# Attention scores from 64-row halves: Q and K turned in float32 two heads at a time, split after the turn

## The chip, the cores and the metric

The kernel runs on one core of a Trainium2 chip. The metric is device time in microseconds, from the profiler's records of whole executions; the median of several runs is compared.

## The reference, cut to what matters

Three stages follow each other: windowed attention with a few sink tokens, a dense feed-forward layer (FFN), and a routed layer of 8 experts.

```python
batch, n_heads, seq, head_dim = (2, 8, 768, 64)
n_sink, window = (4, 128)
scores = scale * np.matmul(q, k.transpose(0, 1, 3, 2))
keep = is_sink | in_window
scores = np.where(keep, scores, -1000000000.0)
scores = scores - np.max(scores, axis=-1, keepdims=True)
a = np.exp(scores)
a = a / (np.sum(a, axis=-1, keepdims=True) + 1e-09)
attn_out = np.matmul(a, v)
x = attn_out.transpose(0, 2, 1, 3).reshape(B * S, H * D)
h = x @ w_in
x = np.maximum(0.01 * h, h) @ w_out
```

Behind it every one of the 1536 tokens goes to the expert of its largest gate logit, while that has room. The weights of the FFN and the experts come as float64.

## The kernel before, in words

**Tiles.** The 1536 tokens are 12 tiles `t` of 128 (6 for each batch entry; `i = t % 6`). Heads go in groups `g` of 4 (two a tile) and in pairs `pr` of 2 (two a group). A score tile of one head holds the keys of the tile itself, of the one before, and of the 4 sinks: `kT` keeps two slots of 128 keys and 4 sink keys each, 264 columns. Tiles 0 and 1 go a plain way of their own (`qk_plain`, `scores_plain` and so on, L624 to L712); tiles 2 to 11 go through `RingAttention` (L394), and of them speaks the change.

**Products in two parts.** To multiply in fp32r, the kernel splits a number into a high part (a copy to fp32r) and a low part (the number less its high part), and sums products of parts. Before the change `high_k` and `low_k` (L146, L151) split K as it lies in memory and put both parts of a head side by side, 64 + 64 columns; `trans_k` (L157) turns these by TensorE (`kps`), so the high part lies on the upper and the low part on the lower 64 rows of `kT`. `high_q`, `low_q` and `trans_q` (L171 to L202) do the same for Q, in both orders, high above low and low above high: for `t < EARLY` (4) by turning 8 tiles a group (`qps`), from there on by turning 4 and copying the halves across on VectorE (L202). `scores` (L487) then needs two matmuls for a head, each over all 128 rows:

```python
for vv in range(2):
    nc.tensor.matmul(out, lhsT=self.qT[t, g][vv][:, h, :], rhs=rhs, start=(vv == 0), stop=(vv == 1))
```

Behind the scores come a copy on ScalarE (`pm`, L506), the window's part on VectorE (L513), the maximum `mx` (L514), exps (L219), the norm (`ri`, L226; POOL, L229), transposes (`pps`, L536) and the product with V: `pv` (L558), where the heads of a pair write the upper and the lower 64 partitions of one PSUM tile in turn, so that each matmul uses 64 columns of the array (`128*64` in the rows; the others say `128*128`).

**What sets the order.** `pipeline` (L333) lays the parts of a group and of a pair on steps: `high_q` and `high_k` three steps ahead of the scores, the low parts two ahead, the turns one ahead, exps one behind, `trans` four and `pv` five behind. From tile 2 on a pair takes two steps. `build` puts these steps between the FFN's work on blocks `j` of 256 tokens: `first` (`hps`, L841), a step, `second` (`y`, L887). Tiles 2, 3 and the start of tile 4 run beside block 0; for that block the FFN uses float32 weights, and VectorE converts 16 weight chunks from float64 (`word`, `cvt`: L779, L783, L789) while DMAs bring them (`rawi`, `rawo`). TensorE, ScalarE, POOL and SP (which issues the DMAs) keep the order of the code. VectorE's order is set by the scheduler that builds the program.

**Buffers.** `kps`, `qps`, `sps` (one a head), `pps` and `ops` take turns in 4 PSUM buffers of tag `att`; a tile is turned into a buffer only when its reader four tiles back is through.

Of the kernel before, what the change touches and what calls it, by code (L numbers as in the profile page):

```python
# [18 lines left out]
P = 128  # L19
# [374 lines left out]
class RingAttention(Attention):  # L394
# [16 lines left out]
    def setup(self):  # L411
        nc = self.nc
        c = self.p["ac"]
        self.R = 2
        self.SC = (self.n_sink + 1) // 2 * 2
        SC = self.SC
        self.W = P + SC
        self.kT = [c.tile([P, self.G, 2, self.W], F32R, name=f"kT{g}") for g in range(self.NG)]
        fill = NEG
        self.qk, self.mp = {}, []  # L420
        if self.plain:
            self.ident_b = self.p["c"].tile([P, P], BF16, tag="c", name="ident_b")
            nc.vector.tensor_copy(self.ident_b, self.ident)
        for t in range(self.plain):

            m = self.p["c"].tile([P, (t + 1) * P], BF16, tag="c", name="mp")
            nc.gpsimd.memset(m, 0.0)
            for x in range(t + 1):
                self.keep_mask(m[:, x * P:(x + 1) * P], (t - x) * P, 0 if x else self.n_sink, fill)
            self.mp.append(m)  # L430
            for g in range(self.NG):
                q = self.p["c"].tile([P, 2, P], F32, tag="c", name="qp")
                k = self.p["c"].tile([P, 2, 2, P], F32, tag="c", name="kz")
                for e in range(2):
                    nc.vector.memset(k[64 - 64 * e:128 - 64 * e, e], 0.0)
                self.qk[t, g] = q, k

        self.m0 = c.tile([P, P], F32, name="m0")
        nc.gpsimd.memset(self.m0, 0.0)
        self.keep_mask(self.m0, 0, self.n_sink, fill)  # L440
        if SC:


            self.m1 = c.tile([P, SC], F32, name="m1")
            self.m2 = c.tile([P, SC], F32, name="m2")
            for m in (self.m1, self.m2):
                nc.gpsimd.memset(m, 0.0)
                if self.n_sink < SC:
                    nc.gpsimd.memset(m[:, self.n_sink:], fill)
            nc.gpsimd.affine_select(out=self.m1, in_=self.m1, pattern=[[-1, SC]],  # L450
                                    compare_op=ALU.is_ge, fill=fill, base=0, channel_multiplier=1)

        self.both = c.tile([P, 2, P], F32, name="both")
        for m, v in ((self.both[:, 0], 1.0), (self.both[:, 1], 0.0)):
            nc.gpsimd.memset(m, v)
            nc.gpsimd.affine_select(out=m, in_=m, pattern=[[1, P]], compare_op=ALU.is_ge, fill=1.0 - v,
                                    base=0, channel_multiplier=-1)

        self.sel = c.tile([P, P], F32, name="sel")
        nc.gpsimd.memset(self.sel, 1.0)  # L460
        nc.gpsimd.affine_select(out=self.sel, in_=self.sel, pattern=[[-1, P]], compare_op=ALU.is_ge, fill=0.0,
                                base=0, channel_multiplier=1)
        self.vs = {}
        if SC:
            self.psk = [c.tile([P, 4, 32], F32, name=f"psk{n}") for n in range(2)]
            for t in self.psk:
                nc.gpsimd.memset(t, 0.0)

    def sink_load(self, b):
# [7 lines left out]
                              in_=self.A["v"][b, e::2, 0:SC, :].rearrange("h s d -> s h d"))  # L477
        self.vs[b] = raw

    def tile_start(self, t):  # L480
        b, i = divmod(t, self.NT)
        if t == self.plain - 1:
            self.load(t + 1, "kqv")
        if self.SC and (b or not self.plain) and self.NT > 1 and i == 0:
            self.sink_load(b)

    def scores(self, t, g, pr):  # L487
        nc = self.nc
        b, i = divmod(t, self.NT)
        W = self.W  # L490
        pm = self.p["pp"].tile([P, 2, W], F32, tag="pm", name="pm")
        mx = self.p["sm"].tile([P, 2], F32, tag="mx", name="mx")
        own = i % 2
        w = W if i else P
        sps = [self.p["ps"].tile([P, 2, W], F32, tag="att", name="sps") for e in range(2)]
        for e in range(2):
            h = 2 * pr + e
            rhs = self.kT[g][:, h, :, :] if i else self.kT[g][:, h, 0, 0:P]
            out = sps[e] if i else sps[e][:, 0, 0:P]
            for vv in range(2):  # L500
                nc.tensor.matmul(out, lhsT=self.qT[t, g][vv][:, h, :], rhs=rhs, start=(vv == 0), stop=(vv == 1))  # L501
        for e in range(2):
            if i == 0:
                nc.vector.tensor_tensor(out=pm[:, e, 0:P], in0=sps[e][:, 0, 0:P], in1=self.m0, op=ALU.add)
            else:
                nc.scalar.copy(pm[:, e, :], sps[e][:, 1 - own, :])  # L506
        if i == 1 and self.SC or i > 1 and self.n_sink < self.SC:
            m = self.m1 if i == 1 else self.m2
            nc.vector.tensor_tensor(out=pm[:, :, P:], in0=pm[:, :, P:],
                                    in1=m.unsqueeze(1).to_broadcast([P, 2, self.SC]), op=ALU.add)  # L510
        if i:
            for e in range(2):
                nc.vector.copy_predicated(pm[:, e, 0:P], self.sel.bitcast(I32), sps[e][:, own, 0:P])  # L513
        nc.vector.reduce_max(mx, pm[:, :, 0:w], axis=AX.X, negate=True)  # L514
        self.pu[t, g, pr] = (pm, mx, w)
# [66 lines left out]
    def steps(self, dense):  # L582

        n, first = self.first_steps()
        return self.pipeline(range(self.plain, self.B * self.NT), dense, n, first,
                             (self.high_k, self.low_k, self.trans_k, self.prep_v))


    def first_steps(self):
# [23 lines left out]
                out.append((u + PT + 1, 0, None, a[0]))  # L613

        for g in range(NG):
            s = base + 2 * g * self.G // 2
            for x in ([0] if self.SC else []) + [self.plain - 1]:
                out += [(s - 3, 0, self.high_k, x, g), (s - 2, 0, self.low_k, x, g), (s - 2, 1, self.trans_k, x, g)]
            out.append((s + 1, 0, self.prep_v, self.plain - 1, g))
        if self.SC:  # L620
            out.append((SINK, 0, self.sink_load, 0))
        return base, out
# [1 line left out]
    def qk_plain(self, t, g):  # L624


        nc = self.nc
        ps = self.p["ps"].tile([P, 4, P], F32, tag="att", name="kps")
        for n, (nm, pr) in enumerate(("kq"[n // 2], n % 2) for n in range(4)):
            x = self.heads(t, g, nm)[:, 2 * pr:2 * pr + 2, :]  # L630
            nc.tensor.transpose(ps[:, n, :], x.rearrange("p a d -> p (a d)"), self.ident)
        q, k = self.qk[t, g]
        nc.vector.tensor_copy(k[0:64, 0], ps[0:64, 0:2, :])
        nc.scalar.copy(k[64:128, 1], ps[64:128, 0:2, :])
        nc.scalar.activation(q, ps[:, 2:4, :], AF.Copy, scale=self.scale)

    def scores_plain(self, t, g):

# [1239 lines left out]
```

## Time and profile before

| | us |
|---|---|
| median of 3 runs | 616.04 |
| lowest and highest run | 615.83, 618.12 |
| the profiled execution, its own time | 618.46 |
| span of its instructions | 616.5 |
| TensorE busy in the span | 586.6 |
| VectorE busy | 382.7 |
| ScalarE busy | 311.9 |
| POOL busy | 179.2 |

PE is TensorE's matmuls and PEld its weight loads, which run beside them; DVE is VectorE, ACT ScalarE. A matmul's row gives a modelled end, and matmuls overlap in the pipeline: what one costs is read from one start to the next. Attention lies between the start and 376 us, the FFN's six blocks between 37 and some 425 us, the experts behind.

### The profile page before, as it was taken

Reading aid. Unit: us, or ns where it says so; the run is one execution under the profiler, and the core shown is the slowest. Engines: PE = TensorE matmul, PEld = TensorE weight load, DVE = VectorE, ACT = ScalarE, POOL = GpSimd, SP = SyncE. Lnnn points to the kernel's source line nnn. Section 1 sums busy time; section 2 is a strip of 40 time slices with the busy share of each in tenths; the row PEclk is TensorE's granted clock in tenths of the full one; section 3 lists DMA queues with packets and bytes.
Section 4 is the critical chain, followed back from the end, with each engine's and each line's share of the span. In section 5 each row is a group of like instructions: output and inputs, shape, how many; then the busy total and the mean of one; then the engine's idle time right before and its main releaser. Section 6 shows DMA issues by size and latency. Waiting matters only on the chain.

```text
span 616.5 us, 11665 instructions
## 1 busy us (share of the span) xinstructions
PE 586.6 (95%) x3889; PEld 502.4 (81%) x3889; DVE 382.7 (62%) x928; ACT 311.9 (51%) x920; POOL 179.2 (29%) x328
## 2 busy tenths in 40 slices
PE   7698998999999999999999999999999999999994
PEld 7575665689889888998889988988798989998783
DVE  4789998377854555555655542266456676655992
ACT  4665555576655455545555433254244544444772
POOL 4425555633342224332422232223110120102110
PEclk9899999999999999999999999999969999999998
DMA  9769989622653402330223015755165856643950
GB/s 244 185 206 249 294 231 269 158 83 53 226 185 108 115 19 69 87 103 19 61 58 98 1 48 164 259 183 165 59 207 172 259 177 204 195 133 111 304 188 12
DMA packets 83564, 91.88 MB, mean 149 GB/s; under 512 B 42964, under 2 KB 51156, under 8 KB 83473
## 3 DMA queue, kind: packets, MB, share of 16 engines
q1 hardware_dynamic: 81488, 85.68, 47.1%
q0 software_dynamic: 1984, 5.13, 2.3%
q8 instruction: 39, 0.64, 0.4%
q14 instruction: 53, 0.43, 0.2%
HBM read 72.01 MB, written 20.09 MB: 149 GB/s over the span
## 4 chain that ended last, share of the span: by engine, by line
PE 70%; DVE 13%; DMA 7%; issue 7%; ACT 3%; POOL 0%; another core or an unknown queue 0%; POOLq 0%; SPq 0%; ACTq 0%; DVEq 0%
PE y L887 18%; PE hps L841 17%; PE ph L1306 10%; PE py L1355 8%; PE ops L568 4%; DVE cvt L789 3%; PE sps L501 3%; DMA out<-ys,gt 2%; DVE word L779 2%; DVE word L783 2%; DMA craw<-in_moe_w 2%; PE lps L972 2%; PE sps L652 1%; PE pps L536 1%; PE kps L163 1%
## 5 line engine op out<-in xcount | busy, mean ns | idle before, releaser
L887 PE MATMUL y<-wh,gp 128*128 128x512 f32 x320 | 115.9, 403 | 0.7 <-ACT gp L867 0.7
L869 POOL TENSOR_TENSOR gp<-g,gp 128x256 fp32r<-128x256 f32 x77 | 56.8, 738 | 197.3 <-ACT gp L867 172.3
L841 PE MATMUL hps<-xth,wh 128*128 128x256 f32 x320 | 92.8, 290 | 0.0
L841 PE MATMUL hps<-xtl,wh 128*128 128x256 f32 x320 | 90.1, 281 | 0.0
L841 PE MATMUL hps<-xth,wl 128*128 128x256 f32 x320 | 89.9, 281 | 0.0
L1170 DVE TENSOR_TENSOR cw<-craw,cw 128x512 fp32r<-128x512 f32 x128 | 83.4, 695 | 9.1 <-ACT cw L1168 7.9
L1168 ACT CAST cw<-craw 128x512 fp32r<-128x512 f32 x112 | 63.4, 621 | 23.7 <-PE py L1355 22.3
L887 PEld LDWEIGHTS y<-wh,gp 128*128 128x128 f32 x320 | 60.0, 188 | 14.3 <-issue 2.7
L857 ACT ACTIVATE g<-hps 128x256 f32<-128x256 f32 x80 | 30.6, 382 | 70.0 <-PE hps L841 65.7
L1355 PE MATMUL py<-cw,ht 128*128 128x512 f32 x264 | 63.9, 397 | 0.2 <-DVE ht L1343 0.2
L841 PEld LDWEIGHTS hps<-xth,wh 128*128 128x128 f32 x320 | 60.3, 188 | 3.3 <-issue 0.9
L841 PEld LDWEIGHTS hps<-xtl,wh 128*128 128x128 f32 x320 | 60.3, 188 | 3.1 <-issue 0.7
L887 PE MATMUL y<-wl,gp 128*128 128x512 f32 x160 | 62.7, 392 | 0.0
L1306 PE MATMUL ph<-xt,cw 128*128 128x256 f32 (+2 forms) x444 | 62.3, 304 | 0.4 <-issue 0.4
L1306 PEld LDWEIGHTS ph<-xt,cw 128*128 128x128 f32 x444 | 61.1, 204 | 0.7 <-issue 0.5
L841 PEld LDWEIGHTS hps<-xth,wl 128*128 128x128 f32 x320 | 60.6, 189 | 0.0
L1355 PEld LDWEIGHTS py<-cw,ht 128*128 128x128 f32 x264 | 49.1, 189 | 11.5 <-DVE ht L1343 0.7
L858 DVE TENSOR_TENSOR g<-hps,g 128x256 f32<-128x256 f32 x80 | 33.4, 418 | 25.6 <-ACT g L857 25.3
L219 ACT ACTIVATE pm<-pm,mx 128x132 f32<-128x132 f32 (+1 forms) x80 | 31.7, 398 | 29.1 <-DVE mx L514 28.9
L867 ACT CAST gp<-g 128x256 fp32r<-128x256 f32 x80 | 33.3, 416 | 23.8 <-DVE g L858 23.6
L1364 POOL DMA_INDIRECT out<-ys,gt x11 | 11.4, 1036 | 114.7 <-DVE ys L1363 114.7
L543 DVE TENSOR_TENSOR pt<-pps,both 128x512 f32<-128x512 f32 x28 | 19.3, 688 | 35.7 <-PE pps L538 35.7
(211 smaller groups left out, 1121.0 us busy)
## 6 DMA issues: line engine op xcount, KB each, us to landing
craw<-in_moe_w SPq DMA_DIRECT2D x128, 256.0 KB, 3.5
rawi<-in_moe_w_in SPq DMA_DIRECT2D x16, 512.0 KB, 5.0
rawo<-in_moe_w_out SPq DMA_DIRECT2D x16, 512.0 KB, 5.4
places<-zero SPq DMA_DIRECT2D x24, 257.0 KB, 5.7
wh<-wscr SPq DMA_DIRECT2D x16, 256.0 KB, 2.9
wl<-wscr SPq DMA_DIRECT2D x16, 256.0 KB, 3.4
xg<-places SPq DMA_DIRECT2D x12, 257.0 KB, 4.4
natv<-in_v SPq DMA_DIRECT2D x12, 256.0 KB, 5.2
```

Of the source, the lines that this page charges most:

```text
L219: nc.scalar.activation(pm[:, e, 0:w], pm[:, e, 0:w], AF.Exp, bias=mx[:, e:e + 1], accum_out=su[:, e:e + 1])
L568: nc.tensor.matmul(ps[64 * e:64 * e + 64, :], lhsT=l, rhs=r, start=(x == 0), stop=(x == len(mm[0]) - 1))
L841: nc.tensor.matmul(ps, lhsT=w, rhs=x, start=(n == 0), stop=(n == len(mm) - 1))
L857: nc.scalar.activation(g, ps, AF.Copy, scale=0.01)
L858: nc.vector.tensor_tensor(out=g, in0=ps, in1=g, op=ALU.max)
L867: nc.scalar.copy(gp[:, 0], g)
L869: eng.tensor_tensor(out=gp[:, 1], in0=g, in1=gp[:, 0].bitcast(F32), op=ALU.subtract)
L887: nc.tensor.matmul(y, lhsT=l, rhs=r, start=(start and n == 0), stop=(stop and n == len(mm) - 1))
L1168: nc.scalar.copy(h, t)
L1170: eng.tensor_tensor(out=l, in0=t, in1=h.bitcast(F32), op=ALU.subtract)
L1306: nc.tensor.matmul(self.ph[f][:, sl], lhsT=self.w[e, "a", h, k][w][:, f * P:(f + 1) * P], rhs=self.xt[:, a, k, sl], start=(m == 0), stop=( ...
L1355: nc.tensor.matmul(self.py[n], lhsT=x, rhs=w, start=(h == 0 and f == 0 and m == 0), stop=(h == self.NH - 1 and f == self.HF - 1 and m == 2))
```

## The change

Q and K of two heads (64 + 64 columns) are turned together in float32, so that one head of a pair lies on the upper and the other on the lower 64 rows. Both are split behind the turn, out of PSUM, into high and low: `qT` holds both parts of a group in one tile, `kT` becomes a high and a low tensor, kTh and kTl. `trans_q` does all of it; `high_k`, `low_k` and `trans_k` are no longer called in the ring, `high_q` does nothing, `low_q` only issues the next load. The scores of a head are three products (high by high, high by low, low by high), each over the head's 64 rows, the two heads in turn. The keys of tile 1 and the sinks of tile 0 are kept from the plain way's own transposes; the second copy of the sinks is made on POOL.

```diff
--- before.py
+++ after.py
@@ -415,7 +415,8 @@
         self.SC = (self.n_sink + 1) // 2 * 2
         SC = self.SC
         self.W = P + SC
-        self.kT = [c.tile([P, self.G, 2, self.W], F32R, name=f"kT{g}") for g in range(self.NG)]
+        self.kT = [[c.tile([P, self.G // 2, 2, self.W], F32R, name=f"kT{a}{g}") for a in "hl"]
+                   for g in range(self.NG)]
         fill = NEG
         self.qk, self.mp = {}, []
         if self.plain:
@@ -477,6 +478,42 @@
                               in_=self.A["v"][b, e::2, 0:SC, :].rearrange("h s d -> s h d"))
         self.vs[b] = raw
 
+    def high_q(self, t, g):
+        pass
+
+    def low_q(self, t, g):
+        if g == self.NG - 1:
+            self.load(t + 1, self.WITH_Q)
+
+    def keep_k(self, t, g, ps):
+
+        nc, SC, i = self.nc, self.SC, t % self.NT
+        hi, lo = ([k[:, :, i % 2, 0:P]] + [k[:, :, r, P:] for r in range(2 if i == 0 and SC else 0)]
+                  for k in self.kT[g])
+        for n, (h, l) in enumerate(zip(hi, lo)):
+            if n == 2:
+                nc.gpsimd.tensor_copy(h, hi[1].bitcast(F32))
+                nc.gpsimd.tensor_copy(l, lo[1].bitcast(F32))
+            elif n or t >= self.plain - 1:
+                src = ps[:, :, 0:SC] if n else ps
+                nc.scalar.copy(h, src)
+                nc.vector.tensor_tensor(out=l, in0=src, in1=h.bitcast(F32), op=ALU.subtract)
+
+    def trans_q(self, t, g):
+
+        nc, NP = self.nc, self.G // 2
+        ps = self.p["ps"].tile([P, 2, NP, P], F32, tag="att", name="qps")
+        for a, nm in enumerate("qk"):
+            for pr in range(NP):
+                x = self.heads(t, g, nm)[:, 2 * pr:2 * pr + 2, :]
+                nc.tensor.transpose(ps[:, a, pr, :], x.rearrange("p a d -> p (a d)"), self.ident)
+        qT = self.p["c"].tile([P, 2, NP, P], F32R, tag="c", name="qT")
+        nc.scalar.activation(qT[:, 0], ps[:, 0], AF.Copy, scale=self.scale)
+        nc.vector.scalar_tensor_tensor(out=qT[:, 1], in0=ps[:, 0], scalar=self.scale, in1=qT[:, 0].bitcast(F32),
+                                       op0=ALU.mult, op1=ALU.subtract)
+        self.qT[t, g] = qT
+        self.keep_k(t, g, ps[:, 1])
+
     def tile_start(self, t):
         b, i = divmod(t, self.NT)
         if t == self.plain - 1:
@@ -493,12 +530,12 @@
         own = i % 2
         w = W if i else P
         sps = [self.p["ps"].tile([P, 2, W], F32, tag="att", name="sps") for e in range(2)]
-        for e in range(2):
-            h = 2 * pr + e
-            rhs = self.kT[g][:, h, :, :] if i else self.kT[g][:, h, 0, 0:P]
-            out = sps[e] if i else sps[e][:, 0, 0:P]
-            for vv in range(2):
-                nc.tensor.matmul(out, lhsT=self.qT[t, g][vv][:, h, :], rhs=rhs, start=(vv == 0), stop=(vv == 1))
+        for n, (a, c) in enumerate(((0, 0), (0, 1), (1, 0))):
+            for e in range(2):
+                r = slice(64 * e, 64 * e + 64)
+                k = self.kT[g][c][r, pr]
+                nc.tensor.matmul(sps[e] if i else sps[e][:, 0, 0:P], lhsT=self.qT[t, g][r, a, pr, :],
+                                 rhs=k if i else k[:, 0, 0:P], start=(n == 0), stop=(n == 2))
         for e in range(2):
             if i == 0:
                 nc.vector.tensor_tensor(out=pm[:, e, 0:P], in0=sps[e][:, 0, 0:P], in1=self.m0, op=ALU.add)
@@ -583,7 +620,7 @@
 
         n, first = self.first_steps()
         return self.pipeline(range(self.plain, self.B * self.NT), dense, n, first,
-                             (self.high_k, self.low_k, self.trans_k, self.prep_v))
+                             (None, None, None, self.prep_v))
 
 
     def first_steps(self):
@@ -613,10 +650,7 @@
                 out.append((u + PT + 1, 0, None, a[0]))
 
         for g in range(NG):
-            s = base + 2 * g * self.G // 2
-            for x in ([0] if self.SC else []) + [self.plain - 1]:
-                out += [(s - 3, 0, self.high_k, x, g), (s - 2, 0, self.low_k, x, g), (s - 2, 1, self.trans_k, x, g)]
-            out.append((s + 1, 0, self.prep_v, self.plain - 1, g))
+            out.append((base + 2 * g * self.G // 2 + 1, 0, self.prep_v, self.plain - 1, g))
         if self.SC:
             out.append((SINK, 0, self.sink_load, 0))
         return base, out
@@ -633,6 +667,8 @@
         nc.vector.tensor_copy(k[0:64, 0], ps[0:64, 0:2, :])
         nc.scalar.copy(k[64:128, 1], ps[64:128, 0:2, :])
         nc.scalar.activation(q, ps[:, 2:4, :], AF.Copy, scale=self.scale)
+        if t == self.plain - 1 or t == 0 and self.SC:
+            self.keep_k(t, g, ps[:, 0:2])
 
     def scores_plain(self, t, g):
```

On TensorE, a group's turn and its first scores (tile 4's first group, in the FFN's block 0; ops is `pv`, hps and y the FFN). Before:

```order
L568 MATMUL ops<-pt,natv 64x128 x4
L568 MATMUL ops<-sp,vsraw 64x128 x2
L163 MATMUL kps<-ident_r,ks 128x128 x4
L197 MATMUL qps<-ident_r,qs 128x128 x4
L841 MATMUL hps<-xth,cvt 128x256 x4
L536 MATMUL pps<-ident,pm 128x128 x2
L538 MATMUL pps<-ident,psk_195 128x128
L501 MATMUL sps<-kT_125,qT 128x264 x4
L887 MATMUL y_723<-cvt,gr 128x512
```

With the change:

```order
L605 MATMUL ops<-pt,natv 64x128 x4
L605 MATMUL ops<-sp,vsraw 64x128 x2
L509 MATMUL qps<-ident,natq 128x128 x2
L509 MATMUL qps<-ident,natk 128x128 x2
L877 MATMUL hps<-xth,cvt 128x256 x4
L573 MATMUL pps<-ident,pm 128x128 x2
L575 MATMUL pps<-ident,psk_197 128x128
L537 MATMUL sps<-kTh_125,qT 128x264 x2
L537 MATMUL sps<-kTl_126,qT 128x264 x2
L537 MATMUL sps<-kTh_125,qT 128x264 x2
L923 MATMUL y_681<-cvt,gr 128x512
```

Four turns of K and four of Q become two of each in float32, and the four score matmuls over all rows are six, in three couples; the rest keeps its place.

Where the ring begins on TensorE (tile 2, behind the plain way's last pv). Before:

```order
L163 MATMUL kps<-ident_r,ks 128x128 x8
L708 MATMUL ops<-pt,natv 64x128 x8
L163 MATMUL kps<-ident_r,ks 128x128 x4
L197 MATMUL qps<-ident_r,qs 128x128 x8
L841 MATMUL hps<-xth,cvt 128x256 x4
L501 MATMUL sps<-kT_125,qT 128x264 x4
```

With the change:

```order
L744 MATMUL ops<-pt,natv 64x128 x8
L509 MATMUL qps<-ident,natq 128x128 x2
L509 MATMUL qps<-ident,natk 128x128 x2
L877 MATMUL hps<-xth,cvt 128x256 x4
L537 MATMUL sps<-kTh_125,qT 128x264 x2
L537 MATMUL sps<-kTl_126,qT 128x264 x2
L537 MATMUL sps<-kTh_125,qT 128x264 x2
```

The turns of K for tiles 0, 1 and 2 and eight of Q become two of Q and two of K; the FFN's first matmuls follow directly.

On VectorE, around the first scores of tile 3 (pm, mx and ri belong to the pair before; word and cvt convert weights). Before:

```order
L779 TENSOR_SCALAR word<-rawo 128x512
L513 COPY_PREDICATED pm<-sel,sps 128x128 x2
L783 SCALAR_TENSOR_TENSOR word<-rawo,word 128x512
L514 TENSOR_REDUCE mx<-pm 128x2
L226 TENSOR_SCALAR ri<-su 128x2
L577 TENSOR_TENSOR xtl<-ops,xth 128x128
L227 RECIPROCAL ri<-ri 128x2
L789 SCALAR_TENSOR_TENSOR cvt<-rawo,word 128x512
L779 TENSOR_SCALAR word<-rawi 128x512
L783 SCALAR_TENSOR_TENSOR word<-rawi,word 128x512
L789 SCALAR_TENSOR_TENSOR cvt<-rawi,word 128x512
```

With the change:

```order
L815 TENSOR_SCALAR word<-rawo 128x512
L550 COPY_PREDICATED pm<-sel,sps 128x128 x2
L819 SCALAR_TENSOR_TENSOR word<-rawo,word 128x512
L551 TENSOR_REDUCE mx<-pm 128x2
L226 TENSOR_SCALAR ri<-su 128x2
L825 SCALAR_TENSOR_TENSOR cvt<-rawo,word 128x512
L512 SCALAR_TENSOR_TENSOR qT<-qps,qT 128x256
L614 TENSOR_TENSOR xtl<-ops,xth 128x128
L227 RECIPROCAL ri<-ri 128x2
L815 TENSOR_SCALAR word<-rawi 128x512
L500 TENSOR_TENSOR kTl_126<-qps,kTh_125 128x2x128
L819 SCALAR_TENSOR_TENSOR word<-rawi,word 128x512
```

The low part of Q (qT) now stands behind the conversion that follows ri, and the low part of K (kTl) behind another; these scores need both. Before, no row of VectorE here belonged to them.

## Rows read from the trace of the kernel before

**Rows 1.** The page, part 1: busy us (share of the span) x instructions, by engine.

```profile
PE 586.6 (95%) x3889; PEld 502.4 (81%) x3889; DVE 382.7 (62%) x928; ACT 311.9 (51%) x920; POOL 179.2 (29%) x328
```

**Rows 2.** Busy time by stage: stretch, its us, then busy us of each engine.

```profile
34.00:106.00 72.00, 63.36 (x361) 44.17 (x358) 64.20 (x129) 40.72 (x136) 34.13 (x53) 1.00 0.90 257
...
130.00:205.00 75.00, 75.00 (x570) 66.79 (x569) 49.08 (x134) 44.78 (x146) 26.13 (x42) 1.00 0.41 130
```

**Rows 3.** The chain that ended last, 20 to 108 us: start us, us, what.

```profile
28.47 0.91 ACT ks L149 x3
...
29.38 0.54 ACT qs L175
...
69.47 0.89 ACT pm L219 x4
...
71.52 0.71 DVE word L779
...
104.95 0.69 DVE qT L202
...
106.40 0.64 PE sps L501 x3
```

**Rows 4.** Waits of PE, 28 to 130 us: us in total, times, longest.

```profile
PE qps L197 <- DVE pm L513: 5.1, 4, 2.5
```

**Rows 5.** PE by line and shape: xcount | busy us, mean ns | idle before.

```profile
L501 PE MATMUL sps<-kT,qT 128*128 128x264 f32 x144 | 27.8, 310 | 2.5 <-DVE qT L202 1.0 <-ACT qT L199 0.9
...
L197 PE MATMUL qps<-ident_r,qs 128*128 128x128 f32 x96 | 11.7, 250 | 5.1 <-DVE pm L513 5.1
```

**Rows 6.** PE in order of time, a score step: start us, us, instruction, count.

```profile
228.80 0.38 PE L536 MATMUL pps<-ident,pm 128*128 128x128 f32 x2
...
229.04 0.73 PE L501 MATMUL sps<-kT,qT 128*128 128x264 f32 x4
229.61 0.39 PE L887 MATMUL y<-wh,gp 128*128 128x512 f32 x1
229.84 0.40 PE L887 MATMUL y<-wl,gp 128*128 128x512 f32 x1
```

**Rows 7.** PE in order of time, a pv step.

```profile
224.52 0.28 PE L841 MATMUL hps<-xtl,wh 128*128 128x256 f32 x1
224.64 0.28 PE L841 MATMUL hps<-xth,wl 128*128 128x256 f32 x1
224.85 0.66 PE L568 MATMUL ops<-pt,natv 128*64 128x128 f32 x8
225.34 0.39 PE L568 MATMUL ops<-sp,vsraw 128*64 128x128 f32 x4
225.65 0.50 PE L887 MATMUL y<-wh,gp 128*128 128x512 f32 x1
225.99 0.40 PE L887 MATMUL y<-wl,gp 128*128 128x512 f32 x1
```

**Rows 8.** PE in order of time, a group's transposes and the y behind them.

```profile
233.33 0.53 PE L163 MATMUL kps<-ident_r,ks 128*128 128x128 f32 x4
...
234.04 0.46 PE L887 MATMUL y<-wh,gp 128*128 128x512 f32 x1
234.34 0.39 PE L887 MATMUL y<-wl,gp 128*128 128x512 f32 x1
```

**Rows 9.** DVE by line and shape: xcount | busy us, mean ns.

```profile
L858 DVE TENSOR_TENSOR g<-hps,g 128x256 f32<-128x256 f32 x80 | 33.4, 418 | 25.6 <-ACT g L857 25.3
...
L182 DVE SCALAR_TENSOR_TENSOR qs<-natq,qs 128x256 fp32r<-128x256 f32 x20 | 9.1, 456 | 1.5 <-ACT qs L175 1.5
```

**Rows 10.** PE in order of time, tile 3's first scores and the y behind.

```profile
71.53 1.12 PE L501 MATMUL sps<-kT,qT 128*128 128x264 f32 x4
72.48 0.59 PE L887 MATMUL y<-cvt,gr 128*128 128x512 f32 x1
```

**Rows 11.** PEld in order of time, the weight loads of that pv step.

```profile
224.84 0.42 PEld L568 LDWEIGHTS ops<-pt,natv 128*64 128x64 f32 x8
```

## The prediction

> **What bounds the kernel now.** I read first the page's busy shares: TensorE is busy for 586.6 of 616.5 us [rows 1]. That is an average, so next the table by stage, where the reader should compare TensorE's busy time with the length of each stretch [rows 2]. From 130 us on it fills the stretch (75.00 of 75.00): there each ns of its queue is a ns of the kernel. From 34 to 106 us it is busy for 63.36 of 72. The chain that ended last says why [rows 3]: in that first stage the chain runs through VectorE, which converts the raw weights (word and cvt steps of some 0.7 us) and does attention between them; at 106.40 us it passes to TensorE (sps). The table of waits names one TensorE wait that matters to the change: 5.1 us in four pieces, qps waiting for a PSUM buffer that VectorE's pm step has not yet released [rows 4].
>
> So the change has two prices: on TensorE's queue after 106 us (10 tiles are turned here, 2 to 11; of their 40 pair steps the 32 of tiles 4 to 11, of their 20 groups the 15 from tile 4's second on), and on VectorE's before that.
>
> **Scores, on TensorE.** The 160 score matmuls (144 of 264 columns and 16 of 128 [rows 5]) become 240, 6 in place of 4 for each pair. What 4 cost: the first transpose starts at 228.80, the first y at 229.61; three transposes of 0.11 (two take 0.38, the last of them 0.27) leave 0.48 us, 0.12 each [rows 6]. The 6 new ones come as three couples, one on the upper and one on the lower 64 rows. No row shows row halves. The nearest is pv, where couples use the left and right 64 columns of the array: 8 matmuls start at 224.85 and the next 4 at 225.34, so after a first couple of 0.16 each couple takes 0.11, which is the time of one matmul [rows 7]. I take couples to overlap by rows as they do by columns: 3 times 0.12, **-0.12 us** a pair.
>
> The same rows show the price of changing the array's shape. Whole-array matmuls of that line come each 0.12 us, but from the last one (224.64) to pv's first it is 0.21; pv's last two couples and the way out take 0.31 (225.34 to 225.65) where two couples would take 0.22; and the first y lasts 0.34 to the next, not 0.23 [rows 6, 7]. All in all 224.64 to 225.99 is 1.35 us for 0.12 + 6 x 0.11 + 0.23 = 1.01: **0.34 us for one visit**, 0.09 on the way in and 0.09 on the way out in which nothing starts, the rest weights whose load is not hidden (0.05 for 64 columns in, 0.11 for 128 out). The new couples load 128 columns each, so in becomes 0.11 too and a visit 0.40. Today's scores pay nothing of this, since transposes, scores and y all use the whole array. Bounds: 0 (row halves need no change of shape) to 0.40; I take 0.40, as the row nearest in kind shows it at every visit.
>
> Here a rule speaks against the change. The Trainium skill, "TensorEngine Tiling (Array Packing)", Tiling Modes, Key Properties, says that changing the tiling mode, rows included, drains the engine. For columns the trace agrees (the 0.21 and the 0.31 above); for rows no run here shows it. By that rule the sum is the one below; without it, the first rival's.
>
> Sum for scores after 106 us: 32 x (0.40 - 0.12) = **+9.0 us**.
>
> **Transposes, on TensorE.** Today a group of 4 heads turns 8 tiles (4 kps, 4 qps; 12 while t is under 4, and k of tiles 0 and 1 as well; 96 are qps [rows 5]). From the first kps to the y behind them it takes 233.33 to 234.04, and that y lasts 0.30, not 0.23 [rows 6, 8]: 0.78 us. The change turns two heads at once in float32, 4 tiles of 0.11 as the pm transposes of [rows 6], which lengthen nothing behind them; with the 0.03 of the way out of pv that stays, 0.47. **15 x -0.31 = -4.7 us.** The extra k turns of tiles 0 and 1 lie before 37 us and belong to the next part.
>
> **The first stage.** There VectorE counts. Gone: the q split (20 x 0.456 us), for t of 4 and more the k split and the two half copies of qT (0.69 each in the chain [rows 3]). New: q and k are both split out of PSUM, 256 columns each; L858, which reads PSUM in the same shape, takes 0.42 [rows 9]. So each of the three groups from tile 2's second to tile 3 gives VectorE 2 x 0.42 - 0.456 = 0.38 more, +1.2 us. At tile 4's first group 1.39 of half copies on the chain are replaced by 0.84 plus, by the new order, part of a 0.7 conversion that now stands ahead of the two splits: -0.4 at best. At the start ks, qs and the q split (0.91 + 0.54 [rows 3], 0.46 [rows 9]) leave the chain; the raw weights' DMA is late next, so I count 1.9 less at most. Together **-1.1 us**. The 5.1 us of TensorE's waits for a PSUM buffer go as well (one buffer a group in place of two or three), but they are not added: TensorE would only arrive sooner at a VectorE that is itself the bound. There is also a new wait: couples 2 and 3 need the low k, and in the new order conversion, q split, word and k split follow the exps (69.47 + 0.89 us [rows 3]), which lets the second couple of tile 3's scores start at some 73.2 us, where all four matmuls began at 71.53 and the y behind them at 72.48 [rows 10]. With two couples more, y comes at some 73.7, 1.2 later. Behind that wait stand y and hps, which have the 5.1 us to give. Bounds of the stage: -4 (all the start's gain, some of the waits) to +3 (the new wait three times at 1.2, nothing gained).
>
> ScalarE loses work in every group, and POOL the early k splits; no engine but TensorE is waited for after 130 us [rows 2], so that is worth nothing. Input DMAs and SP's order stay as they are.
>
> **Sum.** +9.0 - 4.7 - 1.1 = **+3.2 us**. Against the profiled execution's own 618.46 us that is 621.7; that execution lies 2.4 above the median of the three runs, 616.04, against which the forecast is **619.2 us**. A measurement of this kernel can tell about 0.5% (3.1 us) from no change, so this case lies just on that line.
>
> **Rivals.**
> First, *row halves cost no change of shape* (**606 us**, the other side). Place: in and out of every score step. If the weights of a half load behind a whole-array matmul, the visit costs 0 and the sum is 32 x -0.12 - 4.7 - 1.1 = -9.6. It decides from a visit under 0.22 us: there the total falls 3 us below today's. For it: both halves of the rows still feed all 128 columns, unlike pv's couples. Against it: 0.34 at every visit of [rows 7]. Between the two, *only the empty 0.09 in and 0.09 out*, with loads hidden: 32 x 0.06 = +1.9, total -3.9, **612 us**.
>
> Second, *the couples do not overlap* (**630 us**): the change does not do what its order promises. Six matmuls at 0.12 make 0.72, so 32 x (0.72 + 0.40 - 0.48) = +20.5, total +14.7. A milder form has the same price: a half's next weights wait until its matmul is through, a couple takes 0.11 + 0.12 = 0.23, three 0.69, total +13.7. For it: row halves write the same PSUM partitions, which pv's column halves do not. Against it: pv's loads, 8 in 0.42 us, run ahead of their matmuls, 8 in 0.66 [rows 7, 11]. The milder form is how the Trainium skill, "TensorE: Matmul & The Clock Gate", Part 3, The mechanism, puts it: a weight load overlaps a running matmul only when the row groups differ. The column couples here contradict it as a general rule, since their loads overlap on all rows.
>
> Third, *VectorE's first stage* goes to its bounds: +3 makes the forecast 623, -4 makes it 616.
>
> **How the numbers follow.** Forecast with full price of shape 0.50, half of it (the first stage decides) beyond the 0.5% line. No price 0.17; only the empty time 0.18, two thirds of it faster by over 0.5%; no overlap 0.13; an unforeseen gain 0.02. Faster: 0.17 + 0.11 + 0.02 = 0.30. Same: 0.25 + 0.07 = 0.32. Slower: 0.25 + 0.13 = 0.38. The range goes from the first rival with a little of the first stage, 605, to 627, above the forecast's upper bound of 623 and short of no overlap at all. The forecast's own range is 615 to 623.
>
> **What would show it.** Score couples starting together and three in 0.36 us: the overlap is right. From the last transpose to the first couple 0.2 and from first y to second 0.34: the price of shape is right; 0.11 and 0.23: the first rival. Four transposes in 0.44 us. In the first stage the waits of qps for pm gone and waits of sps for VectorE's kTl in their place. Wrong would be the whole argument if TensorE no longer filled the stretches after 130 us, or if the stage before 106 us moved by more than 4 us.

## The result, and the profile after

The changed kernel takes **620.63 us** (median of 11 runs, 618.4 to 624.42) against 616.47 (11 runs, 614.57 to 618.12): ratio 1.007, 95% interval 1.005 to 1.0089. Forecast was 619.2, with 605 to 627 as its range; the result is slower by 0.7%, with an interval that begins at 0.5%. Slower was the likeliest of the three cases, if narrowly.

The profiled execution of the change is one of its shortest (span 616.8 us, own time 618.51), that of the kernel before one of its longest (span 616.5). So their ends lie 0.3 us apart where the medians lie 4.2 apart, and the two traces are compared stretch by stretch.

The page's busy shares of the change (the line that answers to [rows 1]):

```profile
PE 584.9 (95%) x3857; PEld 488.7 (79%) x3857; DVE 362.0 (59%) x906; ACT 290.5 (47%) x868; POOL 172.3 (28%) x328
```

VectorE, ScalarE and POOL each have less to do (VectorE 20.7 us less), and TensorE is as full as before: the kernel did not become shorter by what the side engines were spared.

Busy time by stage, the stretches of [rows 2]: stretch, its us, busy us of PE, PEld, DVE, ACT and POOL, then TensorE's granted clock, DMA share and GB/s.

```profile
34.00:106.00 72.00, 64.21 (x331) 41.79 (x332) 60.71 (x133) 33.64 (x119) 31.44 (x50) 0.95 0.87 260
130.00:205.00 75.00, 75.00 (x562) 64.33 (x561) 45.22 (x132) 40.59 (x138) 25.71 (x42) 1.00 0.45 138
```

From 130 us on TensorE still fills the stretch, so the sum on its queue is the right sum there. TensorE in order of time, the score step that answers to [rows 6] (start us, us, instruction, count):

```profile
227.82 0.38 PE L573 MATMUL pps<-ident,pm 128*128 128x128 f32 x2
228.04 0.27 PE L575 MATMUL pps<-ident,psk 128*128 128x128 f32 x1
228.25 0.39 PE L537 MATMUL sps<-kTh,qT 64*128 64x264 f32 x2
228.47 0.29 PE L537 MATMUL sps<-kTl,qT 64*128 64x264 f32 x2
228.60 0.28 PE L537 MATMUL sps<-kTh,qT 64*128 64x264 f32 x2
228.81 0.50 PE L923 MATMUL y<-wh,gp 128*128 128x512 f32 x1
229.14 0.40 PE L923 MATMUL y<-wl,gp 128*128 128x512 f32 x1
```

From the first transpose to the second y it takes 229.14 - 227.82 = 1.32 us, where it took 229.84 - 228.80 = 1.04: **+0.28 a pair**, the forecast's 0.40 - 0.12. (Over all 30 score steps behind the start of block 1, read from the last transpose to the second y, the mean is +0.26.) The pieces are those of the forecast: 0.21 into the first couple, couples 0.12 apart once the first is through, 0.33 from first y to second.

The turns of a group and the y behind them, same view (they answer to [rows 8]):

```profile
232.61 0.44 PE L509 MATMUL qps<-ident,natq 128*128 128x128 f32 x2
232.89 0.38 PE L509 MATMUL qps<-ident,natk 128*128 128x128 f32 x2
233.02 0.47 PE L923 MATMUL y<-wh,gp 128*128 128x512 f32 x1
233.34 0.39 PE L923 MATMUL y<-wl,gp 128*128 128x512 f32 x1
```

0.41 to the y, and that y lasts 0.32, 0.09 more than 0.23: 0.50 us for 0.78, **-0.28 a group** (forecast -0.31).

Waits of TensorE from 34 to 106 us (us in total, times, longest; [rows 4] held 5.1 us of qps waiting for pm):

```profile
PE sps L537 <- ACT kTh L499: 5.4, 4, 4.3
PE hps L877 <- ACT gr L889: 1.6, 1, 1.6
PE sps L537 <- DVE kTl L500: 0.6, 2, 0.3
```

The wait for pm is gone and a wait for k stands in its place, as foreseen; but it is mostly for the *high* part, which ScalarE writes, and 4.3 us of it come in one piece, at the scores of tile 2's second group.

### The profile page after: what moved, and what is told of

The parts are those of the page before. It is cut to its first block, busy times and chain, and to the rows that moved or that the text cites. A ratio compares the mean times of both kernels' runs of the same rounds, so it can differ in the third digit from the quotient of the medians.

```text
span 616.8 us, 11516 instructions
## 1 busy us (share of the span) xinstructions
PE 584.9 (95%) x3857; PEld 488.7 (79%) x3857; DVE 362.0 (59%) x906; ACT 290.5 (47%) x868; POOL 172.3 (28%) x328
## 5 line engine op out<-in xcount | busy, mean ns | idle before, releaser
L923 PE MATMUL y<-wh,gp 128*128 128x512 f32 x320 | 119.1, 413 | 0.6 <-ACT gp L903 0.6
L1342 PE MATMUL ph<-xt,cw 128*128 128x256 f32 (+2 forms) x444 | 59.3, 295 | 1.1 <-DVE xt L1330 1.1
L1342 PEld LDWEIGHTS ph<-xt,cw 128*128 128x128 f32 x444 | 58.0, 194 | 1.4 <-DVE xt L1330 1.3
```

The lines of the kernel that those rows point to most:

```text
L923: nc.tensor.matmul(y, lhsT=l, rhs=r, start=(start and n == 0), stop=(stop and n == len(mm) - 1))
L1342: nc.tensor.matmul(self.ph[f][:, sl], lhsT=self.w[e, "a", h, k][w][:, f * P:(f + 1) * P], rhs=self.xt[:, a, k, sl], start=(m == 0), stop=( ...
```

## The experiments

Times are medians beside the kernel before on the same chip (616.9 to 617.4 there). Sums over the whole kernel also depend on the granted clock that an execution had in its first 34 us and among the experts, so below some runs are compared at equal mean granted clock. This holds only for edits that leave the clock of the stretches between as it is. For the change these are 618.4 and 618.51 us at 0.987 to 0.988, 620.28 to 621.18 at 0.982 to 0.983 and 624.11 and 624.42 at 0.976.

**e1_by_head: are couples side by side?**

```diff
-        for n, (a, c) in enumerate(((0, 0), (0, 1), (1, 0))):
-            for e in range(2):
+        for e in range(2):
+            for n, (a, c) in enumerate(((0, 0), (0, 1), (1, 0))):
```

> The change with its two score loops exchanged: head by head instead of couple by couple, so that matmuls on the same 64 rows follow each other and nothing else differs. Theory (two matmuls on different rows run side by side): three couples 0.12 us apart become six starts 0.11 to 0.12 us apart, +0.36 us a pair on a full TensorE, 32 pairs: +11.5, some 632 us (1.025 of the kernel before). Rival (the couples were never side by side, their common start in the trace is only how it is recorded): the time stays at 620 to 621 us.

Measured: 623.85 us (4 runs), but at equal clock 622.02 at 0.980 and 623.55 to 624.15 at 0.977, where the change had 622.12 at 0.980 and 624.11 at 0.976: the same, the rival's time. But its reason need not follow. TensorE in order of time, a score step of this kernel:

```profile
205.88 0.38 PE L573 MATMUL pps<-ident,pm 128*128 128x128 f32 x2
206.19 0.40 PE L537 MATMUL sps<-kTh,qT 64*128 64x264 f32 x2
206.42 0.29 PE L537 MATMUL sps<-kTl,qT 64*128 64x264 f32 x2
206.54 0.29 PE L537 MATMUL sps<-kTh,qT 64*128 64x264 f32 x2
206.76 0.50 PE L923 MATMUL y<-wh,gp 128*128 128x512 f32 x1
```

The program has kTh, kTl, kTh of one head and then of the other. The trace has kTh kTh, kTl kTl, kTh kTh, the two of each couple 10 ns apart, in 35 of the 40 steps: TensorE drew the second head's matmuls forward beside the first's. Only around waits does the order of the program show, as at 55 us, where the second matmul waited for kTl and nothing was drawn past it:

```profile
55.48 0.58 PE L537 MATMUL sps<-kTh,qT 64*128 64x264 f32 x1 [4.27 <-ACT kTh L499]
56.07 0.58 PE L537 MATMUL sps<-kTl,qT 64*128 64x264 f32 x1
56.08 0.80 PE L537 MATMUL sps<-kTh,qT 64*128 64x264 f32 x2
```

So by these records the halves of the rows start side by side in either order of the loops, and this test could not tell the theories apart; e2_padded and e6_neighbours together can.

**e2_padded: the same six matmuls without a change of shape.** k's parts are stored for each head on all 128 rows, zeros on the other head's 64:

```diff
-        self.kT = [[c.tile([P, self.G // 2, 2, self.W], F32R, name=f"kT{a}{g}") for a in "hl"]
+        self.kT = [[c.tile([P, 2, self.G // 2, 2, self.W], F32R, name=f"kT{a}{g}") for a in "hl"]
...
-                r = slice(64 * e, 64 * e + 64)
-                k = self.kT[g][c][r, pr]
-                nc.tensor.matmul(sps[e] if i else sps[e][:, 0, 0:P], lhsT=self.qT[t, g][r, a, pr, :],
+                k = self.kT[g][c][:, e, pr]
+                nc.tensor.matmul(sps[e] if i else sps[e][:, 0, 0:P], lhsT=self.qT[t, g][:, a, pr, :],
```

> The change with k's high and low parts of both heads kept on all 128 rows, the other head's 64 rows zero, so that the same six matmuls use the whole array and the array never changes shape for the scores; no two of them can then run side by side. Theory (a visit of another shape costs 0.39 us): six times 0.12 = 0.72 us in place of 0.36 + 0.39 = 0.75, 32 pairs: -1, and the k split in twice as many pieces gives VectorE up to +2 in the first stage: 619 to 622 us; last transpose to first score 0.11 us, first y to second 0.23. Rival (the 0.39 has nothing to do with the shape, it comes with the tiles or their weights): it stays, the couples are lost, +0.36 x 32 = +11.5, some 632 us.

Measured: 625.77 us (4 runs), between the two. A score step of it, same view:

```profile
228.91 0.38 PE L577 MATMUL pps<-ident,pm 128*128 128x128 f32 x2
229.13 0.27 PE L579 MATMUL pps<-ident,psk 128*128 128x128 f32 x1
229.16 0.49 PE L541 MATMUL sps<-kTh,qT 128*128 128x264 f32 x2
229.49 0.40 PE L541 MATMUL sps<-kTl,qT 128*128 128x264 f32 x2
229.73 0.41 PE L541 MATMUL sps<-kTh,qT 128*128 128x264 f32 x2
229.98 0.39 PE L927 MATMUL y<-wh,gp 128*128 128x512 f32 x1
230.21 0.39 PE L927 MATMUL y<-wl,gp 128*128 128x512 f32 x1
```

From the first transpose to the second y: 1.30 us, against 1.32 of the change. The six come one by one, 0.12 apart, and with the whole array y follows y in 0.23 again: 0.36 of lost couples are paid for by 0.39 of shape (-0.03 forecast, -0.02 measured). By itself this step would also fit couples that never overlapped and a change of shape that is free (0.72 against 0.75); e6_neighbours rules that out. The missing 5 us lie elsewhere: the first hps is at 40.77 us (35.98 in the change, 38.05 in e1_by_head), and block 1 begins at 129.10 (119.49 and 121.91). Zeros have to be written there and four pieces of k split; that these are the cause was not tested. From there to the last y it takes 311.57 us, in the change 312.94.

**e3_f32_whole: nothing split.**

```diff
-        for n, (a, c) in enumerate(((0, 0), (0, 1), (1, 0))):
-            for e in range(2):
...
+        for e in range(2):
+            k = self.kT[g][:, e, pr]
+            nc.tensor.matmul(sps[e] if i else sps[e][:, 0, 0:P], lhsT=self.qT[t, g][:, pr, :],
+                             rhs=k if i else k[:, 0, 0:P], start=True, stop=True)
```

> Turned in float32 as in the change, but nothing is split: q and k stay float32, k of both heads on 128 rows with the other head's rows zero, two whole-array float32 matmuls of 264 columns a pair. A float32 matmul of 256 columns (hps from cvt, first stage) starts 0.216 us after the last, so 264 columns take 0.22. Theory (price of the shape 0.39): 0.44 us in place of 0.75, 32 x -0.31 = -9.8, and VectorE is rid of the q split and half of the k work in the first stage, -1 to -2: 609 to 611 us, faster than both kernels. Rival (no price for the shape): 0.44 for 0.36 + 0.39 that stays, +2.6, less the first stage: some 621 to 623 us.

Measured: 627.27 us (4 runs). My price was wrong, not the theory of the shape:

```profile
227.86 0.38 PE L573 MATMUL pps<-ident,pm 128*128 128x128 f32 x2
228.08 0.27 PE L575 MATMUL pps<-ident,psk 128*128 128x128 f32 x1
228.19 1.06 PE L537 MATMUL sps<-kT,qT 128*128 128x264 f32 x4
228.89 0.59 PE L923 MATMUL y<-wh,gp 128*128 128x512 f32 x1
229.31 0.39 PE L923 MATMUL y<-wl,gp 128*128 128x512 f32 x1
```

Two float32 matmuls leave *four* records 0.22 apart: one costs 0.45 us, four times the 0.11 of a rounded one. The 0.216 I had taken from hps<-cvt was half of such a matmul; the records there (128 for 64 matmuls of the program) had told it. With 4 x 0.22 the step is 1.45 us, and 0.11 + 0.89 + 0.23 from the last transpose to the second y (229.31 - 228.08 = 1.23) leaves nothing for a change of shape. The Trainium skill, "FP8 and Floating Point Precision", TensorE Precision Notes, gives true float32 four passes through the array; the 0.45 against 0.11 agrees. Block 1 to the last y takes 315.57 us, 2.6 more than in the change. The experts behind it took 189.7 us in place of 184.4 in this run; the mean granted clock there was 0.967 in place of 0.976, which over that time makes up for 1.7 us by my estimate, and the rest I cannot explain.

**e4_early_turn: the wait of the first stage.** On ScalarE the copy to qT and the high k stand behind the exps; turned one step earlier they stand ahead.

```diff
-                put(mid, s - 1, self.trans_q, t, g)
+                put(mid, s - (2 if t < 5 else 1), self.trans_q, t, g)
```

> The change with the turns of q and k of tiles 2 to 4 issued one step earlier, so that on ScalarE the copy to qT and the high k stand ahead of the exps and do not wait for VectorE's mx. Theory (ScalarE's order makes TensorE's new wait of 4.3 us at 49 to 53 us, and the fall of the granted clock to 0.66 in 50 to 60 us comes from it): the wait of sps for kTh goes, the clock stays at 1.00 there, 2 to 3 us less than the change: 617.5 to 618.5 us, with less spread. Rival (VectorE bounds this stage, the wait only moves to another operand and the stage ends as before): 620 to 621 us.

Measured: **615.46 us** (12 runs, 614.55 to 619.83), 0.999 of the kernel before (0.9971 to 1.001), and 3.7 to 4.7 us under the change at equal clock (614.67 and 614.79 at 0.987, 616.46 and 616.58 at 0.982, 619.74 and 619.83 at 0.976). More than the theory gave, and in another way:

```profile
PE sps L537 <- ACT kTh L499: 3.5, 1, 3.5
PE hps L877 <- ACT gr L889: 1.3, 2, 1.1
PE sps L537 <- DVE kTl L500: 0.3, 1, 0.3
```

The long wait is still there, 3.5 us, and so is the low clock behind it (0.58 from 55 to 60 us). What went are the three short waits for kTh, with those for kTl behind them: from the last transpose to the first y behind tile 3's first scores it takes 0.77 us, in the change 1.89, and at the next two groups 0.77 for 1.86 and 0.77 for 1.55. That is 3.0 us, and block 1 begins 3.1 us sooner (116.42 for 119.49, with the first hps at 36.03 and 35.98). From 60 to 106 us TensorE is busy 46.00 of 46 us, in the change 44.21.

Why the long wait stays, ScalarE's rows show (start us, us, instruction, in brackets the idle time before it and for whom). In the change:

```profile
51.33 0.41 ACT L219 ACTIVATE pm<-pm,mx 128x132 f32<-128x132 f32 x1 [6.14 <-DVE mx L551]
52.13 0.36 ACT L511 ACTIVATE qT<-qps 128x256 fp32r<-128x256 f32 x1
52.98 0.37 ACT L499 CAST kTh<-qps 128x256 fp32r<-128x256 f32 x1 [0.49 <-DVE qT L512]
```

In e4_early_turn:

```profile
45.08 0.38 ACT L511 ACTIVATE qT<-qps 128x256 fp32r<-128x256 f32 x1
51.85 0.37 ACT L499 CAST kTh<-qps 128x256 fp32r<-128x256 f32 x1 [6.39 <-DVE qT L512]
```

In both, the copy to kTh waits for VectorE's split of q (qT, L512). In the change that split waits for the copy to qT, which stands behind exps that had waited 6.1 us for VectorE's mx. In e4_early_turn the copy to qT is early, but the split stands behind VectorE's conversions until 51.41 us, and kTh comes only 1.1 us sooner than in the change. So the long wait goes back to VectorE, through ScalarE. The edit also moves the turns on TensorE and with them VectorE's order; ScalarE's order was not changed by itself.

**e5_warm and e9_warm_14: does the fall of the clock cost anything?** In the change TensorE waits 4.28 us, until 53.40; the granted clock falls (0.66 is a mean of its two levels, 1.2 and 2.4 GHz) and the four y behind come 0.85 to 1.01 us apart instead of 0.43, the lower level:

```profile
50.00:55.00 5.00, 1.60 (x7) 1.06 (x8) 4.28 (x12) 3.18 (x12) 1.05 (x1) 0.66 1.11 291
55.00:60.00 5.00, 5.00 (x12) 2.63 (x12) 4.35 (x10) 1.81 (x8) 3.58 (x7) 0.66 0.85 269
```

Both kernels add matmuls of ident ahead of that pair's scores, whose results the scores overwrite, 36 in e5_warm and 14 in e9_warm_14:

```diff
+        if (t, g, pr) == (2, 1, 0):
+            self.keep_warm(sps[0][:, 0, 0:P], 36)
```

> The change with 36 more matmuls of ident (128 columns, results overwritten by the scores) at the one place where TensorE waited 4.3 us for the high k of tile 2's second group (48.96 to 53.40 us). They compute nothing; 36 x 0.11 = 4.0 us, inside the wait. Theory (that idle time lowers the granted clock, 0.66 from 50 to 60 us, and the y that follow at 0.85 to 1.01 us in place of 0.43 make TensorE late for the rest of the stage): the clock stays at 1.00, y are 0.43 apart, block 1 begins about 3 us sooner, and at the same mean granted clock elsewhere the kernel takes some 617 to 618 us. Rival (VectorE bounds the stage, a slow TensorE there costs nothing): 620 to 621 us.

> The change with 14 matmuls of ident in the wait for tile 2's high k, in place of 36: one such float32 matmul of 128 columns took 0.223 us in e5_warm (two records of 0.112), so 36 were 8.0 us and held the scores up; 14 are 3.1 us, inside the wait. Theory (the fall of the clock behind the idle time makes TensorE late): y behind the scores 0.43 apart, block 1 about 2.5 us sooner than in e1_by_head or the change at the same clock before 34 us, and 617 to 618 us where the other stretches have the clock of the change's runs. Rival (VectorE bounds the stage): 620 to 621 us.

Measured: 619.64 us (11 runs) with 36, which were 8.0 us of float32 and held the scores up (the price of e3 again); 619.46 (12 runs, 616.59 to 622.79) with 14. Against the kernel before these are 1.0034 (1.0012 to 1.0056) and 1.0035 (1.0016 to 1.0053), where the change is 1.007. In e9_warm_14 the windows are as wished up to 60 us, and no longer behind it:

```profile
50.00:55.00 5.00, 4.26 (x35) 3.79 (x35) 4.32 (x12) 2.71 (x10) 0.59 (x1) 1.00 0.86 231
55.00:60.00 5.00, 5.00 (x26) 3.15 (x27) 4.76 (x10) 2.01 (x8) 4.07 (x7) 1.00 1.02 338
70.00:106.00 36.00, 34.27 (x173) 21.87 (x174) 30.02 (x68) 18.69 (x67) 19.05 (x30) 0.95 0.97 261
```

Up to 60 us the clock is 1.00, TensorE does twice the instructions from 55 to 60 us, and y come 0.43 apart. Counted from the first hps (36.44 us here, 35.98 in the change), the pv behind them starts 2.1 us sooner than in the change (58.53 and 60.18 us). The next wait for k, at tile 3's first scores, takes 0.7 of that back: y stands there at 71.57, in the change at 72.57, still 1.5 us ahead. Then this execution had a second fall of the clock, which the change's had not (0.95 from 70 to 106 us, there 1.00), and the lead was gone: from the first hps to block 1 it takes 83.75 us, in the change 83.51.

The fall of the clock at 50 to 60 us comes in every kernel here that has the long wait for k, and in none of the three that fill it with matmuls (e5, e7, e9). So the low clock is not hidden: it cost TensorE 2.1 us, of which the next wait for k covers a part. e5_warm, at 1.00 from the first hps to block 1, shows the same part from the other side: its scores came late, its pv 2.4 us behind that of the change, and from tile 3's first scores on 1.3 us. What is left at the end without a second fall was not measured; the medians, 1.0 us (e5_warm) and 1.2 us (e9_warm_14) under the change, lie between theory and rival. An equal mean clock does not help here, since the edit itself raises the mean.

**e6_neighbours: is the price one of kinds of work, or of changes?** pv comes a step later and between the transposes and the scores.

```diff
+        PV = 6
...
         for t, g, pr, s in units:
-            put(mid, s, self.scores, t, g, pr)
             put(mid, s + 4, self.trans, t, g, pr)
-            put(mid, s + 5, self.pv, t, g, pr)
+        for t, g, pr, s in units:
+            put(mid, s + PV, self.pv, t, g, pr)
+        for t, g, pr, s in units:
+            put(mid, s, self.scores, t, g, pr)
```

> The change with pv moved one step later and put between the transposes and the scores, so that TensorE goes from the column halves of pv straight to the row halves of the scores: three changes of the array's shape a pair in place of four. All matmuls stay. Theory (each change of shape has its own price): the two visits cost 0.39 + 0.34 = 0.73 us in four changes, 0.18 each, 32 x -0.18 = -5.8: 614 to 616 us; the last couple of pv to the first of the scores without the 0.09 of an empty engine on a way out. Rival (each kind of work brings its price with it, whatever stands beside it): 620 to 621 us.

Measured: 616.39 us (10 runs, 612.16 to 618.03), 0.9974 of the kernel before (0.9952 to 0.9996). At equal clock it is 5.6 to 6.4 us under the change (612.16 at 0.987, 616.51 at 0.980, 618.03 at 0.976); forecast was 5.8. A step with pv and scores together:

```profile
143.25 0.27 PE L578 MATMUL pps<-ident,psk 128*128 128x128 f32 x1
143.45 0.66 PE L608 MATMUL ops<-pt,natv 128*64 128x128 f32 x8
143.94 0.39 PE L608 MATMUL ops<-sp,vsraw 128*64 128x128 f32 x4
144.26 0.39 PE L540 MATMUL sps<-kTh,qT 64*128 64x264 f32 x2
144.48 0.28 PE L540 MATMUL sps<-kTl,qT 64*128 64x264 f32 x2
144.60 0.28 PE L540 MATMUL sps<-kTh,qT 64*128 64x264 f32 x2
144.81 0.51 PE L926 MATMUL y<-wh,gp 128*128 128x512 f32 x1
145.16 0.40 PE L926 MATMUL y<-wl,gp 128*128 128x512 f32 x1
```

Column halves (128*64) go straight to row halves (64*128): the way out to the whole array is paid once for both. From the last transpose to the second y it takes 145.16 - 143.25 = 1.91 us. Less 0.11 for the transpose, 6 x 0.11 for pv, 3 x 0.12 for the couples and 0.23 for y, 0.55 is left: three changes at 0.18, where the two visits alone cost 0.39 + 0.34 in four. The price belongs to each change of shape. If the couples did not overlap, the scores would take 0.72 and 0.19 would be left for all three, less than the 0.34 that pv's visit costs by itself [rows 7]; so they overlap. The Trainium skill, "TensorEngine Tiling (Array Packing)", Tiling Modes, Key Properties, says that changing the mode drains the engine; for rows, too, the trace agrees that a change has a price, here some 0.18 us.

That the whole kernel gained just the forecast's 5.8 is in part luck. From the start of block 1 to the last y the trace has 309.59 us, 3.4 less than the change, with 1.8 us of new idle time of TensorE in it (73.17 busy of 75 us from 130 us on): 5.2 us of the array's time, the 0.18 a step. Another 2.4 us come from the stage before, 81.07 us from the first hps to block 1 for 83.51, where the three short waits for kTh are gone, as in e4_early_turn.

**e7_early_warm** (early turns and 28 matmuls of ident together).

> Early turns of tiles 2 to 4 and the ident matmuls in the wait that is left there (28, 3.1 us of 3.7) together. Theory (the order on ScalarE and the clock each cost their own time): 615.5 of the early turns less some 3 for the clock, 612 to 613 us, faster than the kernel before by about 4 us. Rival (both remove the same thing, TensorE's lateness, and then VectorE bounds): 615 to 616 us.

Measured: 627.66 us (4 runs). Its 28 matmuls take 6.2 us, not 3.1, so it tests neither theory. The experts took 191 us in its profile, at a mean granted clock of 0.940 (0.976 and 184.4 us in the change). Inconclusive.

**e8_early_neighbours: the two gains together.** The edits of e4 and e6.

> Early turns of tiles 2 to 4 and pv beside the scores, together. At the same mean granted clock the first took 3.8 to 4.5 us from the change, the second 5.6 to 6.3; the one lies before 106 us, the other mostly behind it. Theory (two separate costs of the change: its order in the first stage, and its changes of the array's shape): 620.6 - 4.2 - 5.9, some 610 to 611 us, 1% faster than the kernel before. Rival (the first stage of the second has its own order, in which the early turns find nothing to save): 614 to 616 us.

Measured: **611.01 us** (6 runs, 610.24 to 615.31), **0.9903** of the kernel before (0.9873 to 0.9932). The change can be made to pay, by 1%. The number is the theory's, the profile is the rival's: from the first hps to block 1 it takes 81.00 us (e6_neighbours 81.07), from there to the last y 309.75 (309.59). On top of e6 the early turns found nothing to save in this stage, since both edits remove the same three short waits. At equal clock the kernel is 7.8 us under the change (610.67 and 610.68 at 0.987), where the two gains together would be 9.3 to 11.1, and 1.5 us under e6_neighbours. The two profiles differ ahead of the first hps (37.48 and 39.09 us) and among the experts (mean clock 0.990 and 0.974); where the 1.5 us come from stays open.

## Why the prediction was right

- **Scores, +9.0.** Right in mechanism and nearly in size: couples overlap (e2 and e6 together), and a visit costs 0.40 as forecast (0.39 by e2's balance). The mean of +0.26 makes 7.9 us for the 30 steps behind the start of block 1; the four steps of tile 6, whose scores have 128 columns, became longer by 0.23. The first rival (no price for row halves) falls by e2, e3 and e6, the second (no overlap) by e6. The first rival's turning point is nearer 0.21 than 0.22: 32 x (0.22 - 0.12) - 5.8 is -2.6, not -3.
- **Transposes, -4.7.** 15 x -0.28 = -4.2; the y behind them is held up a little longer than counted.
- **Sum behind 106 us.** +4.3 was forecast. From the start of block 1 to the last y the trace gives 312.94 us (119.49 to 432.43) against 309.28 (122.02 to 431.30), +3.7 with 30 of the 32 steps and 14 of the 15 groups (by the steps 7.9 - 3.9 = 4.0).
- **First stage, -1.1.** Near to it where the clock is alike, but not for my reasons; that is luck. e1_by_head does there what the change does, and it and the kernel before both had 0.78 from 20 to 34 us: block 1 begins at 121.91 and 122.02, **-0.1**. The start, from which I hoped up to 1.9, lost 1.0 (first hps at 38.05 for 37.04); the rest of the stage gained 1.1. In the change's own profile, with 1.00 from 20 to 34 us, block 1 begins 2.5 us sooner than before; that is the execution's luck. +3.7 and -0.1 make 3.6 of the 4.2 between the medians; what is left is within the spread of the experts' part.
- **The step that failed** is the new wait. It was priced at 1.2 us, for the low k on VectorE at tile 3's first scores, and left out of the sum because the 5.1 us of waits that go were to cover it. At that place it measured 1.1 us, kTh and kTl together (1.1 and 0.8 at the next two groups). What the prediction had not seen is tile 2's second group: 4.3 us in one piece, for the high k. ScalarE writes that behind exps that waited 6.1 us for VectorE's mx, and behind VectorE's q split, and the low clock that followed cost TensorE another 2.1 us (e9). I had priced the split by its VectorE half alone. That block 1 still began 0.1 us sooner at like clock is a balance of these losses against the 5.1 us of waits for pm that went and against VectorE's lighter load; it came near the forecast without its terms.

e4's early turns took away the three short waits, 3.0 us up to block 1. That is not the loss forecast on TensorE's queue, which stays: from block 1 to the last y e4 takes 313.09 us, the change 312.94. The long wait stays argued in part: the rows show that kTh waits for VectorE's q split, but why it does (both read the PSUM buffer qps, different halves of it) is not shown, and moving that split ahead of the conversions was not tried.

## What to carry to other kernels

Count the changes of the array's shape, not the matmuls: halves that run two at a time broke even on TensorE's queue only when put beside other work in halves (e6: 309.59 us from block 1 to the last y, 309.28 before). When a conversion moves from one engine to two, look at what stands ahead of each half in order on each of them. When two edits each gain, see whether they remove the same wait before adding them (e8). Before trusting a duration, compare a group's number of records with the number of matmuls that the program has.

## What was not expected of the hardware

- Matmuls on the other 64 rows are taken out of the program's order: written head by head, they ran in couples 10 ns apart in 35 of 40 steps (e1). The Trainium skill, "TensorE: Matmul & The Clock Gate", Part 2, Step-by-step, says that matmuls stay in program order and only weight loads are drawn forward; for row halves this trace differs, and the measurement decides.
- A mean clock of 0.66 from 50 to 60 us, behind a wait of 4.28, cost TensorE 2.1 us; the next wait for k covered 0.7 of it (e9).
- A float32 matmul takes 0.45 us for 264 columns and 0.22 for 128, while a float32 transpose of 128 takes 0.11 (e3, e5).
